# Another order for the first batch's steps, and nine unread products before the first expert tile

## The chip, the cores and the metric

The kernel runs on one core of a Trainium2 chip. The core has TensorE (PE, matrix products and transposes, with its weight loads shown apart as PEld), VectorE (DVE), ScalarE (ACT) and GpSimd (POOL). SyncE (SP) issues all the DMAs of this kernel. Every engine works through its own list of instructions in order and waits where a semaphore tells it to. The metric is the device time of one execution in microseconds (us).

## The reference, cut to what matters

Inputs are `q`, `k`, `v` of 8 batches x 8 heads x 576 rows x 64, `p` of 8 x 8 x 32 x 64, and the weights `w_a`, `w_b` (512 x 1536) and `w_out` (1536 x 512), all float32.

```python
p_packed = sm_attn(p, k, v)            # first scores: p @ k, softmax, times v
out = sm_attn(q, p_packed, p_packed)   # second scores: q @ pp, softmax over 32, times pp
x = out.transpose(0, 2, 1, 3).reshape(4608, 512)
return (x @ w_a) * (x @ w_b) @ w_out
```

## The kernel before

**Batches.** The eight batches are worked off one after the other. A batch has two attention stages, each in two halves (`e` = 0 and 1), and then the feed-forward part. Instead of forming the attention output, the kernel multiplies `pp` (the packed result of the first softmax) by a chunk of `w_a` and `w_b` ("pp @ w", `g_tiles`, L332), and multiplies that by the second softmax's weights `a2` (`mm1`, L351). There are six chunks of two f-tiles, so twelve f-tiles (`ft`) in a batch. Every operand of L351 is split into a high and a low part (`a_hi`, `a_lo`, `ghi`, `glo`), and three of the four products of parts are made, 12 matmuls for each half of an f-tile. ACT copies the first half out of PSUM (L363), DVE multiplies it with the second (L366), ACT and POOL split the result (L370, L86). Then `mm2` (L377) multiplies by `w_out`.

**The first scores** of batch 0 need k turned: five loads-and-turns `k0` to `k4` (`turn_first`), where `k0`, `k1` come from the first load (part 0), `k2`, `k3` from the second (part 1) and `k4` from the third (part 2), the same for q. A turn is four (for `k4`, `q4` eight) PE transposes into a bank and a copy by DVE or ACT; the string `TURN` says which. `S0`, `S1` are the score products of the two halves (L247), `r0`, `r1` the next steps of their softmax (L253 to L287), `P0` turns `pp` (L236, L237).

**The second scores** are `s0` and `s1`, one step at each mention: 1 the products (L297), 2 a transpose and a maximum on DVE (L302, L304), 3 the subtraction (L307), 4 the exponential on ACT (L309), 5 the sums and the reciprocal on DVE (L312 to L314) and the multiplication (L315), 6 a transpose on DVE (L318) and the high part on ACT (L319), 7 the low part on DVE (L86, `a_lo`). Steps 3 and the multiplication of 5 run on `eng`, in batch 0 on DVE for `s0` and on POOL for `s1`.

**The weights** come as 36 pieces of 512 KB: 24 of `w_a` and `w_b`, 12 of `w_out`. A piece is converted in three steps: A (the high word, ACT, L189), B (the low word, L194 or L197, on ACT, DVE or POOL as the digit of `WAYS` says: 0, 1, 2), C (both joined, DVE, L200). Twelve buffers hold pieces; a C frees one and issues the next load. D splits a `w_out` piece (ACT L225, POOL L86). Pieces 0 to 3 make chunk 0, 4 to 7 chunk 1 and so on; C makes a `w_out` piece in one single buffer, `wo_f`, which D empties.

**The order** is written out by hand. `FIRST` is the order of the first DMAs, `START` the steps up to the first f-tile, and the strings of `PLAN_0` the steps that stand after each half f-tile of batch 0 (24 slots) and after its `w_out` rounds. `Lp`, `Lk`, `Lq`, `Lv` issue the loads of the next batch. `g` in `START` is pp @ w of the first chunk. Later batches follow `PLAN`, which the change leaves alone. The PSUM pool `m` that `bank_pair()` gives out has two buffers.

Of the kernel before, what the change touches and what calls it, by code (L numbers as in the profile page):

```python
# [19 lines left out]
def tile_packed_attn_gated_ffn(  # L20
# [20 lines left out]
    nc = tc.nc  # L41
    B, H, S, D = q.shape
# [29 lines left out]
    ident = const.tile([P, P], F32, name="ident")  # L72
# [12 lines left out]
    def lo_part(dst, src, hi, eng=nc.vector):  # L85
        return eng.tensor_tensor(out=dst, in0=src, in1=hi.bitcast(F32), op=ALU.subtract)  # L86

    def bank():
        return ps_x.tile([P, 512], F32, name="x")

    def bank_pair(s=False):
        return ps_s.tile([P, 2, 512], F32, name="s") if s else ps_m.tile([P, 2, 512], F32, name="m")

    def work(b, name, shape, tag=None):
        if b == 0:
            return scratch.tile(shape, F32, name=name)
        return wk.tile(shape, F32, name=tag, bufs=2 if tag == "t1" else 1)
# [17 lines left out]
    def turn(key, b, i):  # L115

        t = nats.pop((key, b, i))
        xT = ld.tile([P, R, HS], F32, name=f"xT{i}")
        nc.vector.transpose(out=xT.rearrange("p h t -> p (h t)"), in_=t.rearrange("p h x d -> p (h x d)"))  # L119
        xTs.setdefault((b, key), []).append(xT)  # L120
# [3 lines left out]
    firsts = {}  # L124
# [12 lines left out]
    def turn_first(key, n):  # L137

        if (0, key) not in xTs:
            pool = scratch if key == "q" else ld  # L140
            xTs[0, key] = [pool.tile([P, R, HS], F32, name=f"xT{i}") for i in range(2)]
        copy = (nc.vector.tensor_copy, nc.scalar.copy)[int(TURN["kq".index(key) * 5 + n])]
        x = bank_pair()[:, 0, :] if n in (2, 3) else bank()
# [36 lines left out]
    def xT_cols(b, key, u, h, cols=slice(0, HS)):  # L180
        return xTs[b, key][h // R][64 * u:64 * u + 64, h % R, cols]
# [49 lines left out]
    def turned(dst, src, back=0):  # L231

        tp = bank()
        cols = src.rearrange("p e d -> p (e d)")
        for i in range(2):
            nc.tensor.transpose(tp[:, P * i:P * i + P], cols[:, 64 * (i ^ back):64 * (i ^ back) + P], ident)  # L236
        nc.vector.tensor_copy(out=dst.rearrange("p i r j -> p (i r j)"), in_=tp[:, 0:2 * P])  # L237
# [52 lines left out]
    def stage2(b, e):  # L290

        TU = 2 * XH
        hi, lo = (t[:, e, :].rearrange("p (x u l) -> p u x l", u=2, l=TL) for t in (a2_hi, a2_lo))
        x = bank_pair(b == 1 or e == 0)
        for r in range(R):
            for u in range(2):
                nc.tensor.matmul(  # L297
                    out=x[J * r:J * r + J, u, 0:HS], lhsT=ppT[64 * u:64 * u + 64, 1 if u ^ e else 2 * (b % 2), r, :],
                    rhs=xT_cols(b, "q", u, 2 * r + e), start=True, stop=True)
        yield  # L300
        s2 = work(b, f"s2_{e}", [P, TU, J], "t1")
        nc.vector.transpose(out=s2.rearrange("p (u x) j -> p u (x j)", u=2), in_=x[:, :, 0:HS])  # L302
        mx = sm.tile([P, TU], F32, name="mx")
        nc.vector.tensor_reduce(out=mx, in_=s2, axis=AX, op=ALU.max)  # L304
        yield
        eng = nc.gpsimd if b or e else nc.vector
        eng.tensor_tensor(out=s2, in0=s2, in1=mx.unsqueeze(2).broadcast_to([P, TU, J]), op=ALU.subtract)  # L307
        yield
        nc.scalar.activation(out=s2, in_=s2, func=AF.Exp, scale=scale)  # L309
        yield  # L310
        sum2 = sm.tile([P, TU], F32, name="sum2")
        nc.vector.tensor_reduce(out=sum2, in_=s2, axis=AX, op=ALU.add)  # L312
        nc.vector.tensor_scalar(out=sum2, in0=sum2, scalar1=1e-9, scalar2=None, op0=ALU.add)
        nc.vector.reciprocal(out=sum2, in_=sum2)  # L314
        eng.tensor_tensor(out=s2, in0=s2, in1=sum2.unsqueeze(2).broadcast_to([P, TU, J]), op=ALU.mult)  # L315
        yield
        a2f = work(b, f"a2f_{e}", [P, 2, XH, TL], "t2")
        nc.vector.transpose(out=a2f.rearrange("p u x l -> p (u x l)"), in_=s2.rearrange("p x j -> p (x j)"))  # L318
        nc.scalar.copy(out=hi, in_=a2f)  # L319
        yield  # L320
        lo_part(lo, a2f, hi)
        yield
# [97 lines left out]
    def emit(b, plan, tasks={}):  # L420

        for name in plan.split():
            if name in tasks:
                next(tasks[name], None)
                continue
            if name in "ABCD":
                convert(name)
                continue
            what, e = name[:-1], int(name[-1])
            n = b + (e // 2 if b or what[0] == "L" else 0)  # L430
            if n >= B:
                continue
            if what == "S":
                if e == 0:
                    st[b] = [stage1(b, 0), stage1(b, 1), stage2(b, 0), stage2(b, 1)]
                next(st[b][e])
            elif what == "s":
                next(st[b][2 + e], None)
            elif what == "r":
                next(st[b][e], None)  # L440
            elif what == "T":
                turned(pT, p_nat.pop(n))
            elif what == "P":
                turned(ppT[:, b % 2:b % 2 + 2], pp.pop(b), b % 2)
            elif what in ("k", "q"):
                turn(what, n, e % 2) if b else turn_first(what, e)
            elif what == "Lk":
                load(k, "k", n, e % 2)
            elif what == "Lq":
                load(q, "q", n, e % 2)  # L450
            elif what == "Lv":
                load_v(n, e % 2)
            elif what == "Lp":
                load_p(n)

    st = {}

    FIRST = ("p0 k0 k1 k2 q2 q0 v0 q1 v1 w1 w1 w1 w1 w1 w1 w1 w1 w1 w1 w1")
    START = ("T0 k0 k4 k1 k3 k2 q0 S0 S1 r0 q1 r1 r1 r0 r0 r1 r0 q2 r1 q3 P0 q4 A s0 A B s0 s0 B s1 s0 B s1 A s1 "
             "s0 C B Lp2 A C s1 s1 B A B B C B A C A s0 s1 s0 C Lk2 C B g A Lv2 A A C A B C B s1 C B A B Lk3 C A "  # L460
             "s1")
    WAYS = ("000000022220202120112012011200110102")
    TURN = ("1001111101")

    PLAN = (" | S0 | r0 |  | r0 | r0 |  | r0 Lv1 |  | S1 | r1 | q0 Lk2 | r1 |  |  | r1 q1 Lk3 |  | r1 Lv2 |  |  | "
            "T2 P0 |  |  | s0 s0 s1 g s0 |  | s1 | Lp4 s0 s1 s1 k2 | s0 | s0 | s1 s0 | s1 Lq2 | s1 | k3 Lq3")
    PLAN = dict(enumerate(PLAN.split("|")))
    PLAN_0 = ("B | C C | C A B A | C C A B B | A C A | k0 | A | B Lq0 B B | B C A C T0 A | C Lp2 C k1 | B A A | S0 "
# [3 lines left out]
    PLAN_0 = dict(enumerate(PLAN_0.split("|")))  # L472

    pieces = [(c, n) for c in range(NC) for n in range(4)] + [(NC, f) for f in range(NFT)]
# [2 lines left out]
    def load_pieces(n):  # L477

        for _ in range(n):
            if unloaded and len(raws) + len(wo_hi) + len(wo_f32) < NFT:  # L480
                c, r = unloaded.pop(0)
                if c < NC:
                    load_w(c, r)
                else:
                    load_wout(r)

    def convert(x):

        if x == "D":
            if wo_f32:  # L490
                split_wout(wo_f32.pop(0))
                load_pieces(2)
            return
        if not to_do[x]:
            return
        c, n = to_do[x].pop(0)
        if (c, n) not in raws:
            load_pieces(1)
        raw = raws[c, n]
        if x == "A":  # L500
            high_word(raw)
        elif x == "B":
            low_word(raw, int(WAYS[pieces.index((c, n))]))
        else:
            assert len(to_do["A"]) <= len(to_do[x]) and len(to_do["B"]) <= len(to_do[x])
            if c < NC:
                i, rr = divmod(n, 2)
                both_words(w_ab[:, c, 2 * rr:2 * rr + 2, 2 * P * i:2 * P * i + 2 * P], raw)
            else:
                t = sm.tile([P, DO], F32, name="wo_f32", bufs=1)  # L510
                both_words(t, raw)
                wo_f32.append(t)
            del raws[c, n]
            load_pieces(2)

    def next_g(b):

# [4 lines left out]
    ep(tc.manual_schedule(engines={ET.PE, ET.DVE, ET.Activation, ET.Pool, ET.SP}))  # L522
    for name in FIRST.split():
        what, i = name[0], int(name[1])
# [9 lines left out]
    tasks = {"g": next_g(0)}  # L534
    emit(0, START, tasks)
    drain(tasks["g"])
# [6 lines left out]
    for b in range(B):  # L543
        plan = dict(PLAN if b else PLAN_0)
        slot, tasks = [0], {"g": next_g(b + 1)}
# [73 lines left out]
```

## Time and profile before

| | |
|---|---|
| median of 3 runs | 748.11 us (747.31 to 749.12) |
| the profiled execution | 747.04 us |
| its span, first to last instruction | 745.3 us |
| busy in the span | PE 719.9 (97%), DVE 308.8 (41%), ACT 281.4 (38%), POOL 214.1 (29%) |
| mean granted clock of TensorE | 0.993 |

Busy is the time in which an engine had an instruction under way; for PE that is not its peak rate, since matmuls overlap. The time outside the span is 1.74 us. The shares are averages over a start in which PE waits a lot and a long rest in which it does not.

### The profile page before, as it was taken

Reading aid. Unit: us, or ns where it says so; the run is one execution under the profiler, and the core shown is the slowest. Engines: PE = TensorE matmul, PEld = TensorE weight load, DVE = VectorE, ACT = ScalarE, POOL = GpSimd, SP = SyncE. Lnnn points to the kernel's source line nnn. Section 1 sums busy time; section 2 is a strip of 40 time slices with the busy share of each in tenths; the row PEclk is TensorE's granted clock in tenths of the full one; section 3 lists DMA queues with packets and bytes.
Section 4 is the critical chain, followed back from the end, with each engine's and each line's share of the span. In section 5 each row is a group of like instructions: output and inputs, shape, how many; then the busy total and the mean of one; then the engine's idle time right before and its main releaser. Section 6 shows DMA issues by size and latency. Waiting matters only on the chain.

```text
span 745.3 us, 13719 instructions
## 1 busy us (share of the span) xinstructions
PE 719.9 (97%) x5844; PEld 602.9 (81%) x5844; DVE 308.8 (41%) x487; ACT 281.4 (38%) x494; POOL 214.1 (29%) x155
## 2 busy tenths in 40 slices
PE   5589899999999999999999999999999999999998
PEld 4278777888888888889788897888888888888887
DVE  2898856355303553244702446045520455123200
ACT  3777743444114531344203542055311553034300
POOL 0395754334103340133301333033400334023300
PEclk9799999999999999999999999999999999999999
DMA  8999952432510414014230242314050100100011
GB/s 255 362 255 256 284 100 54 88 67 54 92 41 24 71 43 91 30 45 90 47 74 15 55 80 47 76 33 73 24 106 29 33 1 2 43 15 1 1 29 43
DMA packets 171005, 58.30 MB, mean 78 GB/s; under 512 B 140608, under 2 KB 158784, under 8 KB 170944
## 3 DMA queue, kind: packets, MB, share of 16 engines
q1 hardware_dynamic: 170944, 57.43, 31.6%
q8 instruction: 46, 0.75, 0.4%
q14 instruction: 15, 0.12, 0.0%
HBM read 47.97 MB, written 9.44 MB: 77 GB/s over the span
## 4 chain that ended last, share of the span: by engine, by line
PE 91%; DVE 3%; DMA 1%; POOL 1%; issue 1%; ACT 1%; SPq 0%; DVEq 0%; POOLq 0%; ACTq 0%
PE m L377 40%; PE m L351 39%; PE x L332 6%; PE s L281 1%; PE s L247 1%; DVE w_ab L200 1%; PE s L297 1%; DMA kn<-in_k_dram 1%; PE s L271 1%; POOL wo L86 1%; DMA raw<-in_moe_w_b_dram 1%; DVE wo_f L200 1%; PE x L236 0%; PE m L297 0%; PE m L147 0%
## 5 line engine op out<-in xcount | busy, mean ns | idle before, releaser
L377 PE MATMUL m<-wo,h_hi 128*128 128x512 f32 (+1 forms) x888 | 268.8, 385 | 0.8 <-DVE asb L366 0.8
L86 POOL TENSOR_TENSOR h_lo<-asb,h_hi 128x576 fp32r<-128x576 f32 x96 | 138.6, 1444 | 411.5 <-ACT h_hi L370 411.3
L377 PEld LDWEIGHTS m<-wo,h_hi 128*128 128x128 f32 x888 | 164.2, 188 | 40.0 <-DVE t L302 5.0
L366 DVE TENSOR_TENSOR asb<-m,asb 128x576 f32<-128x576 f32 x96 | 72.6, 756 | 279.9 <-PE m L351 277.5
L351 PE MATMUL m<-a_hi,ghi 128*128 128x288 f32 x768 | 171.0, 304 | 2.4 <-ACT asb L363 1.7
L377 PE MATMUL m<-wo,h_lo 128*128 128x512 f32 (+1 forms) x444 | 170.4, 384 | 0.0
L351 PE MATMUL m<-a_lo,ghi 128*128 128x288 f32 x768 | 163.9, 295 | 0.9 <-DVE a_lo L86 0.9
L351 PEld LDWEIGHTS m<-a_hi,ghi 128*128 128x128 f32 x768 | 122.1, 188 | 39.7 <-issue 16.8
L351 PE MATMUL m<-a_hi,glo 128*128 128x288 f32 x768 | 133.4, 295 | 1.0 <-DVE glo L86 1.0
L351 PEld LDWEIGHTS m<-a_lo,ghi 128*128 128x128 f32 x768 | 123.5, 188 | 1.1 <-DVE a_lo L86 1.1
L370 ACT CAST h_hi<-asb 128x576 fp32r<-128x576 f32 x96 | 64.7, 674 | 143.0 <-DVE asb L366 143.0
L351 PEld LDWEIGHTS m<-a_hi,glo 128*128 128x128 f32 x768 | 112.7, 188 | 1.2 <-DVE glo L86 1.2
L377 PEld LDWEIGHTS m<-wo,h_lo 128*128 128x128 f32 x444 | 83.4, 188 | 16.7
L86 DVE TENSOR_TENSOR glo<-x,ghi 128x512 fp32r<-128x512 f32 x96 | 61.7, 684 | 52.7 <-ACT ghi L338 52.7
L363 ACT COPY asb<-m 128x576 f32<-128x576 f32 x96 | 61.6, 641 | 39.2 <-PE m L351 31.5
L332 PE MATMUL x<-w_ab,ppT 64*32 64x512 f32 x768 | 57.9, 606 | 7.9 <-DVE w_ab L200 7.9
L412 ACT COPY asb<-m 128x512 f32<-128x512 f32 x24 | 14.1, 587 | 134.2 <-PE m L377 133.4
L338 ACT CAST ghi<-x 128x512 fp32r<-128x512 f32 x96 | 51.4, 588 | 5.9 <-PE x L332 5.9
L119 DVE STREAM_TRANSPOSE xT<-nat 128x1152 f32<-128x1152 f32 x28 | 38.3, 1367 | 0.0
L412 ACT COPY wo_f<-m 128x512 f32<-128x512 f32 x11 | 6.5, 588 | 55.4 <-PE m L377 55.4
L332 PEld LDWEIGHTS x<-w_ab,ppT 64*32 64x32 f32 x768 | 13.6, 106 | 15.9 <-issue 12.3
L194 POOL TENSOR_SCALAR raw<-raw 128x512 uint32<-128x512 uint32 x11 | 23.7, 2157 | 0.9
(106 smaller groups left out, 407.2 us busy)
## 6 DMA issues: line engine op xcount, KB each, us to landing
nat<-in_k_dram SPq DMA_DIRECT2D x56, 144.0 KB
nat<-in_q_dram SPq DMA_DIRECT2D x56, 144.0 KB
vt<-in_v_dram SPq DMA_DIRECT2D x28, 256.0 KB
raw<-in_moe_w_a_dram SPq DMA_DIRECT2D x12, 512.0 KB
raw<-in_moe_w_b_dram SPq DMA_DIRECT2D x12, 512.0 KB
raw<-in_moe_w_out_dram SPq DMA_DIRECT2D x12, 512.0 KB
out_dram<-asb SPq DMA_DIRECT2D x17, 256.0 KB
out_dram<-wo_f SPq DMA_DIRECT2D x10, 256.0 KB
```

The costliest lines, as they stand in the source:

```text
L86: return eng.tensor_tensor(out=dst, in0=src, in1=hi.bitcast(F32), op=ALU.subtract)
L119: nc.vector.transpose(out=xT.rearrange("p h t -> p (h t)"), in_=t.rearrange("p h x d -> p (h x d)"))
L194: (nc.vector if way == 1 else nc.gpsimd).tensor_scalar(out=low, in0=low, scalar1=2.0 ** -29, scalar2=7.0, op0=ALU.mult, op1=ALU.min)
L200: nc.vector.scalar_tensor_tensor(out=dst.bitcast(U32), in0=raw[..., 1], scalar=3, in1=raw[..., 0], op0=ALU.logical_shift_left, op1=ALU.bit ...
L332: nc.tensor.matmul(out=gps[e][J * r:J * r + J, :], lhsT=ppT[rows, 2 * (b % 2), r, :], rhs=w_ab[rows, c, r, :], start=True, stop=True)
L338: nc.scalar.copy(out=ghi[:, e], in_=gps[e])
L351: nc.tensor.matmul(out=ps[:, half, 0:HS], lhsT=gt[:, kt, i, :], rhs=at[:, kt, HS * half:HS * half + HS], start=(n == 0 and kt == 0), stop= ...
L363: nc.scalar.copy(out=asb, in_=pa[:, :, 0:HS])
L366: nc.vector.tensor_tensor(out=asb, in0=pb[:, :, 0:HS], in1=asb, op=ALU.mult)
L370: nc.scalar.copy(out=hh, in_=flat)
L377: nc.tensor.matmul(out=o[:, cols], lhsT=ht[:, c0:c0 + P], rhs=wt[:, cols], start=(ft == 0 and n == 0), stop=(ft == NFT - 1 and n == 2))
L412: nc.scalar.copy(out=ob, in_=o)
```

## The change

`FIRST`, `START`, `PLAN_0`, `TURN` and `WAYS` get other contents, the engine of the subtraction and multiplication of the second softmax is read from a string `SUBS` (batch 0: half 0 on POOL, half 1 on DVE; batch 1 as before), and a step `W` issues nine products of the identity with the first 512 columns of the first k load as it came from memory, between the products of the second scores and `g`. Nobody reads their result.

```diff
-        eng = nc.gpsimd if b or e else nc.vector
+        eng = nc.vector if b < 2 and SUBS[2 * b + e] == "1" else nc.gpsimd
...
+            if name == "W":
+                warm()
                 continue
...
-    FIRST = ("p0 k0 k1 k2 q2 q0 v0 q1 v1 w1 w1 w1 w1 w1 w1 w1 w1 w1 w1 w1")
-    START = ("T0 k0 k4 k1 k3 k2 q0 S0 S1 r0 q1 r1 r1 r0 r0 r1 r0 q2 r1 q3 P0 q4 A s0 A B s0 s0 B s1 s0 B s1 A s1 "
-             "s0 C B Lp2 A C s1 s1 B A B B C B A C A s0 s1 s0 C Lk2 C B g A Lv2 A A C A B C B s1 C B A B Lk3 C A "
-             "s1")
-    WAYS = ("000000022220202120112012011200110102")
-    TURN = ("1001111101")
+    FIRST = ("p0 k0 k2 k1 q0 v0 q1 v1 q2 w1 w1 w1 w1 w1 w1 w1 w1 w1 w1 w1")
+    START = ("T0 k0 k4 k1 k3 k2 q0 S0 S1 r0 r1 q1 r1 r0 r0 r1 r0 q2 r1 q3 q4 P0 s0 B s1 W A s0 B A A s0 s0 B s1 C "
+             "A s1 B s0 C s1 A s1 C B B Lp2 C A B A s0 s1 B C B B s0 B g A C A A s1 Lv2 Lk2 C C A A C B B Lk3 C s1")
+    WAYS = ("000000022220202120012012011200010010")
+    TURN = ("0001110101")
+    SUBS = ("0100")
...
-    PLAN_0 = ("B | C C | C A B A | C C A B B | A C A | k0 | A | B Lq0 B B | B C A C T0 A | C Lp2 C k1 | B A A | S0 "
-              "B | B A C r0 | r0 C | B A | C C C | B r0 D A | C S1 A D B | A Lq1 C B B D | r1 C | A D A | r0 | C A "
-              "D B | B r1 B B r1 A B C Lv1 |  |  | q0 C q1 r1 D A Lk2 A | C D P0 Lv2 C D | s0 s0 Lk3 A C | T2 s1 s1 "
-              "D | B s0 | D A | B s0 s0 C | k2 D s1 Lp4 s0 k3 | s1 s1 |  | s0 Lq2 Lq3 s1 s1")
+    PLAN_0 = ("A | C C | B A B A | B C B C C | A A | C | B | C B A T0 k0 Lp2 A | A A B B C Lq0 | C C k1 | A B A | "
+              "S0 B | B A r0 | C C C | B A Lq1 |  | C C B r0 r0 D A A | S1 C D | B C B B A D | r1 C | A A D | r0 T2 "
+              "|  | q0 B r1 C B D r1 C |  | A | D B C Lv1 A r1 | A B D Lk2 B C B q1 D Lk3 A A P0 | C s0 s0 D C Lp4 "
+              "A B | s1 s0 | Lv2 | D | s0 s1 s0 | k2 s0 s1 C k3 | s1 |  | Lq2 D s0 s1 s1 Lq3 s1")
...
+    def warm(n=9):
+
+        x = bank_pair()[:, 0, :]
+        t = firsts["k", 0].rearrange("p h t -> p (h t)")
+        for _ in range(n):
+            nc.tensor.matmul(out=x, lhsT=ident, rhs=t[:, 0:512], start=True, stop=True)
```

## Rows read from the trace of the kernel before

**Rows 1.** Stretches of the span: length, each engine's busy time, clock, DMA share, GB/s

```profile
22.69:36.97 14.28, 5.39 (x48) 1.27 (x49) 13.00 (x20) 11.12 (x21) 5.62 (x4) 0.64 1.01 355
...
43.78:64.85 21.07, 20.71 (x187) 17.22 (x179) 20.05 (x27) 15.75 (x28) 16.23 (x9) 1.00 0.98 265
...
92.68:745.30 652.62, 649.37 (x5135) 548.00 (x5135) 242.13 (x385) 220.40 (x382) 167.05 (x122) 1.00 0.23 49
```

**Rows 2.** Timeline of PE, the start to the second scores: start, length, instruction

```profile
10.26 1.11 PE L147 MATMUL x<-ident,kn 128*128 128x128 f32 x4
11.17 1.91 PE L147 MATMUL m<-ident,kn 128*128 128x128 f32 x8
12.88 0.73 PE L147 MATMUL x<-ident,qn 128*128 128x128 f32 x4
13.53 0.77 PE L247 MATMUL s<-xT,pT 64*32 64x288 f32 x10
...
22.69 0.86 PE L297 MATMUL s<-xT,ppT 64*32 64x288 f32 x16 [0.35 <-ACT xT L154]
...
24.33 0.67 PE L297 MATMUL m<-xT,ppT 64*32 64x288 f32 x3 [0.31 <-issue]
```

**Rows 3.** Chain of waits that ended last: start, length, what; to 23 us

```profile
3.79 5.38 DMA kn<-in_k_dram
...
14.72 0.77 DVE nmx L253
...
16.60 0.47 ACT xT L149
...
22.37 0.28 ACT xT L154
```

**Rows 4.** Timeline of DVE, then of POOL, from the second softmax on

```profile
29.74 1.28 DVE L200 SCALAR_TENSOR_TENSOR w_ab<-raw 128x512 uint32<-128x512 uint32 x2
...
32.11 2.18 DVE L200 SCALAR_TENSOR_TENSOR w_ab<-raw 128x512 uint32<-128x512 uint32 x2
...
36.40 1.72 DVE L200 SCALAR_TENSOR_TENSOR w_ab<-raw 128x512 uint32<-128x512 uint32 x2
...
39.25 1.27 DVE L200 SCALAR_TENSOR_TENSOR w_ab<-raw 128x512 uint32<-128x512 uint32 x2
...
32.34 1.40 POOL L315 TENSOR_TENSOR s<-s,sum 128x576 f32<-128x576 f32 x1 [3.65 <-ACT raw L189]
33.83 11.32 POOL L194 TENSOR_SCALAR raw<-raw 128x512 uint32<-128x512 uint32 x5
```

**Rows 5.** Timeline of PE and ACT, pp @ w of the first chunk, first f-tile

```profile
32.89 3.39 PE L332 MATMUL x<-w_ab,ppT 64*32 64x512 f32 x16 [7.88 <-DVE w_ab L200]
36.97 0.54 PE L351 MATMUL m<-a_hi,ghi 128*128 128x288 f32 x2 [0.69 <-ACT ghi L338]
...
41.25 0.53 PE L351 MATMUL m<-a_lo,ghi 128*128 128x288 f32 x2 [0.87 <-DVE a_lo L86]
...
43.78 0.53 PE L351 MATMUL m<-a_hi,ghi 128*128 128x288 f32 x2
...
35.02 1.33 ACT L319 CAST a_hi<-a2f 128x576 fp32r<-128x576 f32 x2 [2.19 <-DVE a2f L318]
```

**Rows 6.** Timelines of SP and ACT: loads of pieces 21 on, and their first use

```profile
57.25 0.76 SPq L210 DMA_DIRECT2D raw<-in_moe_w_a_dram  x1
...
63.30 0.68 ACT L197 ACTIVATE raw<-raw 128x512 uint32<-128x512 uint32 x1
```

**Rows 7.** Timeline of PE, two later waits, and of DVE before the second

```profile
82.83 0.53 PE L351 MATMUL m<-a_hi,ghi 128*128 128x288 f32 x2 [1.32 <-ACT asb L363]
...
92.68 0.50 PE L377 MATMUL m<-wo,h_hi 128*128 128x512 f32 x1 [0.78 <-DVE asb L366]
...
90.06 1.90 DVE L200 SCALAR_TENSOR_TENSOR wo_f<-raw 128x512 uint32<-128x512 uint32 x1 [1.02 <-POOL wo L86]
91.89 0.74 DVE L366 TENSOR_TENSOR asb<-m,asb 128x576 f32<-128x576 f32 x1
```

More of the change, by code (lines that the diff above doesn't have):

```diff
@@ L425, in emit @@
                 continue
+            if name == "W":
+                warm()
+                continue
             if name in "ABCD":
@@ L467, in tile_packed_attn_gated_ffn @@
     PLAN = dict(enumerate(PLAN.split("|")))
-    PLAN_0 = ("B | C C | C A B A | C C A B B | A C A | k0 | A | B Lq0 B B | B C A C T0 A | C Lp2 C k1 | B A A | S0 "
[3 rows of a table removed]
+    PLAN_0 = ("A | C C | B A B A | B C C B C | A A | C | B | C B A T0 k0 Lp2 A | A A B B C Lq0 | C C k1 | A B A | "
[3 rows of a table added]
     PLAN_0 = dict(enumerate(PLAN_0.split("|")))
```

## The prediction

> **What bounds the kernel now.** I read the table of stretches first. From 92.68 us on, PE is busy 649.37 of 652.62 us [rows 1]: the last of batch 0 and seven batches whose plan is not touched. Nothing can be won there; an advance reached by then goes whole into the end, and so does a delay. Between the start of the second scores (22.69) and the first f-tile (36.97) PE is busy 5.39 of 14.28 us and DVE 13.00, so DVE sets the pace and PE waits for it; the mean granted clock is 0.64 there. From 43.78 to 64.85 PE has 20.71 of 21.07 us and DVE 20.05: both nearly full, so DVE can't catch up on much [rows 1]. The chain of waits shows what sets the start: the third k load, which lands at 3.79 + 5.38 = 9.17, then turns and scores on PE, the maximum on DVE at 14.72, a copy on ACT between two exponentials (16.60, 0.47), and at 22.37 the copies of `q4` [rows 3]. Last the timelines: pp @ w waits 7.88 us for the third conversion C, and the first f-tile stops again for `ghi` and for the second low part, at 41.25 [rows 5]. So I follow one checkpoint after another and ask how much earlier each is reached.
>
> **The start.** Before, `k4` waits for the third k load, and `k1`, which is behind it on PE, begins at 10.26 [rows 2]. With the small load ahead of the second one, `k4` can fill the idle time that was there, and `k1` waits for the second load, which then lands last of the three. Whatever their order, the three were all there at 9.17 [rows 3]; so `k1` begins at about 9.3, 0.95 earlier. Eight transposes took 11.17 to 12.88, 0.214 us each, and the four of `q0` 0.65 together (12.88 to 13.53), so the rate doubled within them [rows 2]. If the clock rises at the same moment, `q0` is slower by 0.2: the first scores begin 0.75 earlier, at 12.8. I take 0.8, since they then also stop less for a copy. Bounds: 0.4, if the second load is late by as much; 2.2, if the clock rises as early as `k1`, which saves 0.107 on each of the 12 to 16 transposes. The q load that moves behind v is first used at `q4`, whose copies came at 22.37, 13 us after the k loads, and the piece loads behind it keep their place: nothing.
>
> `q1`'s copy goes from ACT to DVE, behind both maxima. It stood between the exponentials for 0.47 [rows 3]; the second maximum takes over as the limit, so I take 0.35 (0 to 0.47). `P0` behind `q4` means that the copy of `ppT` on DVE ends this part and not `q4`'s copies: 0.2 lost (0 to 0.5). The second scores begin 0.8 + 0.35 - 0.2 = 0.95 earlier, at 21.75. Call that moment X; before it is 22.69.
>
> **The nine products.** A float32 product shows as two matmuls (the 8 of L332's loops are x16 [rows 5]), so W is 18 matmuls of 512 columns. No row has one. Turns of the same full array take 0.214 for 128 columns at what their later doubling shows to be the 1.2 GHz level, so 0.107 at 2.4 and four times that, 0.43, for 512: 7.7 us. I take 8.0, with starts between; at the lower level it would be 15.4. W follows the products of `s1`, which before ended at 24.33 + 0.67 = X + 2.3 [rows 2], so it ends at X + 10.3. The cover is the softmax on DVE: the fourth C ends at X + 10.9 (below), and pp @ w needs the third and fourth. W's bank was read long before (`q3`'s copy), and the first f-tile gets that of `s1`, which DVE has read by then. What W gives is the clock: the second-scores stretch showed 0.64 [rows 1], and pp @ w took 3.39 us in it. But ACT had both `a_hi` casts to do until 35.02 + 1.33 = 36.35, and pp @ w was over at 36.28 [rows 5], so the faster products are worth about 0 on the path; they keep the earlier f-tile from starting at half clock. I cost W at 0. The casts end 2.06 behind the fourth C (36.35 - 34.29), and pp @ w takes at most half of 3.39 at the higher level, so W may end as late as X + 10.9 + 2.06 - 1.7 = X + 11.3; past that it costs what it exceeds it by.
>
> **The second softmax.** DVE has the same steps up to the fourth C. Before, this pair of conversions took 2.18 (32.11 to 34.29 = X + 11.6), while the pair at 29.74 took 1.28: the second one ran beside POOL's multiplication (32.34, 1.40) and ended after it [rows 4]. After, POOL multiplies half 0 and begins when DVE has just begun its second conversion, as at 32.34, and behind that stands half 1's sum; DVE then does half 1's subtraction and multiplication. That saves 0.9, and 0.2 comes back because POOL's conversions, which began right behind its multiplication (33.83), now begin sooner and run beside the third and fourth C (pairs beside them: 1.72 and 1.27, against 1.28 alone [rows 4]). Sum 0.7; bounds 0, if the multiplication catches another conversion, and 0.9. POOL is slower at the two steps, but half 1's steps on DVE cover it: its result is due only after the fourth C. The fourth C: X + 10.9 = 32.65.
>
> **The first f-tile.** Before, two pairs of conversions (36.40, 1.72, and 39.25, 1.27) stood on DVE between the transposes and the second low part, for which PE stood still at 41.25 [rows 4, 5]. After, two conversions, one pair less: 1.3 (bounds 0, if ACT's copies end last, and 1.7). So the checkpoint at 41.25 comes 0.95 + 0.7 + 1.3 = 2.95 earlier.
>
> **What is late next.** The conversions that were put off stand, four in a row, ahead of the first gate (L366). PE wants the bank that it frees only in the second half of the next f-tile, 1.0 for pp @ w and 1.6 behind the first; four conversions take 2.6 to 3.4 by the pairs. I take 0.3 lost (0 to 0.8). SP: piece 17 goes ahead of the k and v loads of batch 1, and pieces 21 on stand behind the second k load as before; 21 was issued at 57.25 and first used at 63.30 [rows 6]. All of that SP list is freed by conversions that come 1 to 2 us earlier, and a use that comes 3 earlier eats some of the 6 between: 0.2 lost (0 to 1). Of the later waits the one at 82.83 stays, since a D still stands ahead of ACT's copies. The one at 92.68 came from a conversion of 1.90 ahead of the last gate (90.06, 91.89) [rows 7]; its slot is now empty, so most of 0.78 goes: 0.6 (0 to 0.78).
>
> **The sum.** 2.95 - 0.3 - 0.2 + 0.6 = 3.05, say 3.1. The profiled execution took 747.04 (span 745.3 and 1.74 around it): 743.9. The median of the runs shown is 1.07 above it, so the median after should be 748.11 - 3.1 = 745.0.
>
> **Rivals.** *DVE gives it back.* Where DVE is 20.05 of 21.07 us busy [rows 1], PE can keep only what DVE itself gained, 0.95 + 0.7, and reordering conversions gains DVE nothing: 1.65, or 0.8 less with the gate late by its bound: 746.5 to 747.3. For it speaks DVE's share, against it that PE's waits there were short.
> *Nothing arrives.* The pieces come too late, or the chain through the single `wo_f` buffer (C on DVE, D on ACT and POOL) sets when batch 0 ends and doesn't move: within 1 us of 748.1. Against it: C there follows a gate, and the gate follows PE.
> *Slower: W is not hidden.* If W runs at the 1.2 GHz level, 15.4, it ends at X + 17.7, 6.4 us after its limit, and 3.3 remain after what was won: 751.4. For it speaks that the clock did fall in this stretch; against it, that PE idled 7.88 us in it, and that W starts without a gap behind the scores. It decides once W ends after X + 11.3 + 3.1 = X + 14.4.
> *More.* The clock rises at `k1` (1.4 more), or the waits behind 43.78 shrink as well: 743.6 and below.
> *The clock rule.* Before, the rate of turns doubled while PE had done nothing but turns from 10.26 on [rows 2]. If turns did not raise the clock, the first scores and `q1`'s turns would begin at half rate, about 1 us more by the 0.65 to 0.77 that such groups take: 746.0. The Trainium skill's page "TensorE: Matmul & The Clock Gate", section on PE-mode transpose, says that transposes do not bring the full clock; by that rule the sum would be 746.0, but these rows do not agree with it.
>
> **How the numbers follow.** Forecast (2.1 to 4.1 won) 0.46, more 0.10, DVE gives it back 0.22, the clock rule 0.03, nothing 0.10, slower 0.09. About 0.2% or 1.5 us is what a measurement of this kernel can tell from no change. Faster by more: 0.46 + 0.10 + half of 0.22 + 0.02 = 0.69; within: the other half, 0.01 and 0.10 = 0.22; slower: 0.09. The range, 743.0 to 747.6, leaves out the slower case, half of nothing and some of more.
>
> **What would show it.** `k1`'s turns at 9.3; the second scores near 21.7; 18 matmuls of 0.43 to 0.49 behind them, over before pp @ w, and a clock of 1.0 throughout; the fourth C near 32.7; the first f-tile near 35 and its second low part near 38; no wait over 0.3 at the first `mm2` product. A pp @ w that stands behind W, a first gate after 42, or ACT waiting for piece 21 would make it wrong.

## The result, and the profile after

The changed kernel takes 739.62 us in the median of 4 runs (739.47 to 741.35), beside 747.93 us of the kernel before (747.31 to 749.12): a ratio of 0.9892 with an interval of 0.9873 to 0.9911. So it is 8.3 us faster, where 3.1 were forecast and 743.0 was the lower end of the range. The profiled executions stand 7.34 apart (747.04 and 739.7, spans 745.3 and 737.9). One run of experiment 5, of 1189.78 us, stands far off all others and moves the median of that experiment by 0.14.

The table of stretches of the kernel after, at the stretches of [rows 1]: from the second scores to the first f-tile, from the second f-tile to the start of the seventh, and the last 652.62 us.

```profile
core 0: us, PE busy (x) PEld busy (x) DVE busy (x) ACT busy (x) POOL busy (x), PEclk, DMA share, GB/s
22.08:35.09 13.01, 11.36 (x67) 4.35 (x67) 11.96 (x21) 10.60 (x20) 7.47 (x5) 1.00 1.06 387
40.35:60.16 19.81, 19.69 (x182) 17.06 (x178) 17.52 (x27) 16.27 (x29) 16.14 (x9) 1.00 1.04 254
85.28:737.90 652.62, 649.43 (x5136) 547.91 (x5134) 241.24 (x385) 222.96 (x386) 164.47 (x121) 1.00 0.24 51
```

The last stretch, counted back from the end, is PE's 649 of 652.62 us as before, so the advance was there when it began. The second one is 1.26 us shorter than before's 21.07, though nothing was forecast for it. The granted clock is 1.00 in all three; before it was 0.64 in the first.

The timeline of PE after, at the checkpoints of [rows 2, 5]: start, length, instruction, and in brackets the wait ahead of it.

```profile
9.32 1.11 PE L147 MATMUL x<-ident,kn 128*128 128x128 f32 x4
...
11.93 1.06 PE L147 MATMUL x<-ident,qn 128*128 128x128 f32 x4
12.92 1.00 PE L247 MATMUL s<-xT,pT 64*32 64x288 f32 x24
13.74 0.90 PE L247 MATMUL m<-xT,pT 64*32 64x288 f32 x24
...
22.08 0.72 PE L297 MATMUL s<-xT,ppT 64*32 64x288 f32 x16 [0.61 <-DVE ppT L237]
...
23.90 7.99 PE L524 MATMUL m<-kn,ident 128*128 128x512 f32 x18
32.04 1.57 PE L332 MATMUL x<-w_ab,ppT 64*32 64x512 f32 x16 [0.15 <-DVE w_ab L200]
35.09 0.54 PE L351 MATMUL m<-a_hi,ghi 128*128 128x288 f32 x2 [1.48 <-ACT ghi L338]
...
37.68 0.53 PE L351 MATMUL m<-a_lo,ghi 128*128 128x288 f32 x2 [0.27 <-DVE a_lo L86]
...
40.35 0.53 PE L351 MATMUL m<-a_hi,ghi 128*128 128x288 f32 x2
```

L524 is `warm()`: 18 matmuls in 7.99 us. They fill the time in which pp @ w waited 7.88 before, and it starts 0.15 behind them. The waits of [rows 7] have no counterpart: behind 37.68 the largest wait of PE in batch 0 is one of 0.12, ahead of 43.92.

The timelines of DVE and POOL after, which answer to [rows 3, 4] (the first line is the maximum of the first scores, 14.72 before), the last two lines being POOL's and SP's (piece 21, [rows 6]):

```profile
14.12 0.76 DVE L253 TENSOR_REDUCE nmx<-s 128x1 f32<-128x576 f32 x1 [1.25 <-PE s L247]
...
31.22 1.28 DVE L200 SCALAR_TENSOR_TENSOR w_ab<-raw 128x512 uint32<-128x512 uint32 x2
...
37.54 3.43 DVE L200 SCALAR_TENSOR_TENSOR w_ab<-raw 128x512 uint32<-128x512 uint32 x4
40.90 0.74 DVE L366 TENSOR_TENSOR asb<-m,asb 128x576 f32<-128x576 f32 x1
...
28.54 1.41 POOL L315 TENSOR_TENSOR s<-s,sum 128x576 f32<-128x576 f32 x1 [2.83 <-DVE sum L314]
...
54.50 0.76 SPq L210 DMA_DIRECT2D raw<-in_moe_w_a_dram  x1
```

The third and fourth C (31.22) now take 1.28, the multiplication on POOL (28.54) being over before they begin; the four conversions that were put off (37.54) stand ahead of the first gate at 40.90.

The account below is taken from PE's starts in the two timelines (only the fourth C's end is DVE's); "c2" is pp @ w of the third chunk, and so on. Its last column is what the prediction's sum put there.

| stretch | before | after | gained | forecast |
|---|---|---|---|---|
| to the second scores (X) | 22.69 | 22.08 | 0.61 | 0.95 |
| X to the end of the fourth C | 11.60 | 10.42 | 1.18 | 0.7 |
| to the second low part | 6.96 | 5.18 | 1.78 | 1.3 |
| to c2 (50.35, after 47.31) | 9.10 | 9.63 | -0.53 | -0.3 |
| to c3 (58.97, 55.12) | 8.62 | 7.81 | 0.81 | -0.2 |
| to c4 (68.23, 63.55) | 9.26 | 8.43 | 0.83 | 0 |
| to c5 (76.87, 72.19) | 8.64 | 8.64 | 0 | 0 |
| to the first `mm2` product (90.97, 84.85) | 14.10 | 12.66 | 1.44 | 0 |
| to batch 1's first pp @ w (126.12, 118.78) | 35.15 | 33.93 | 1.22 | 0.6 |
| to the end (745.3, 737.9) | 619.18 | 619.12 | 0.06 | 0 |

Up to the second low part 3.57 came instead of 2.95, and behind it 3.83 instead of 0.1. The larger half of the surprise lies where the forecast had left the profile as it was. Of the 1.22, 0.3 is no gain: the two turns of p for batch 2, which took 0.31 of PE there before (110.65 to 110.96), now stand in the stretch ahead, at 80.93.

Two of the four waits that are gone are in [rows 7]. The other two are the 0.36 at 55.38 and c3, which took 1.91 instead of 1.09 within PE's own row. The timelines of the kernel before up to c3 (PE, DVE, POOL), and then around the wait at 82.83 (DVE, POOL, ACT):

```profile
55.38 0.53 PE L351 MATMUL m<-a_hi,ghi 128*128 128x288 f32 x2 [0.36 <-ACT asb L363]
...
58.97 1.91 PE L332 MATMUL x<-w_ab,ppT 64*32 64x512 f32 x16
...
56.87 2.53 DVE L200 SCALAR_TENSOR_TENSOR w_ab<-raw 128x512 uint32<-128x512 uint32 x2
59.33 0.41 DVE L237 COPY pT<-x 128x256 f32<-128x256 f32 x1
...
57.07 1.78 POOL L86 TENSOR_TENSOR h_lo<-asb,h_hi 128x576 fp32r<-128x576 f32 x1 [1.75 <-ACT h_hi L370]
...
78.71 1.90 DVE L200 SCALAR_TENSOR_TENSOR wo_f<-raw 128x512 uint32<-128x512 uint32 x1 [1.11 <-POOL wo L86]
...
78.63 1.44 POOL L86 TENSOR_TENSOR h_lo<-asb,h_hi 128x576 fp32r<-128x576 f32 x1
...
80.65 0.62 ACT L225 CAST wo<-wo_f 128x512 fp32r<-128x512 f32 x1 [1.59 <-DVE wo_f L200]
...
82.13 0.65 ACT L363 COPY asb<-m 128x576 f32<-128x576 f32 x1
```

In both places a conversion on DVE begins beside a `TENSOR_TENSOR` of POOL and ends 0.55 after that has ended (59.40 after 58.85, 80.61 after 80.07): 1.78 for the second of the pair and 1.90, where 0.65 to 0.69 is usual. Behind the first stands the copy of `pT` (59.33), which frees the bank that c3 wants (its weight loads wait 0.7 for that copy); behind the second stands D on ACT (80.65), and behind D the copy L363 (82.13) for which PE waits at 82.83. The same in the kernel after (DVE, POOL, ACT):

```profile
53.16 0.42 DVE L237 COPY pT<-x 128x256 f32<-128x256 f32 x1
...
69.39 0.69 DVE L200 SCALAR_TENSOR_TENSOR wo_f<-raw 128x512 uint32<-128x512 uint32 x1
...
72.96 0.73 DVE L200 SCALAR_TENSOR_TENSOR wo_f<-raw 128x512 uint32<-128x512 uint32 x1 [0.34 <-POOL wo L86]
...
73.40 1.58 POOL L86 TENSOR_TENSOR h_lo<-asb,h_hi 128x576 fp32r<-128x576 f32 x1 [0.47 <-ACT h_hi L370]
...
73.73 0.62 ACT L225 CAST wo<-wo_f 128x512 fp32r<-128x512 f32 x1 [0.41 <-DVE wo_f L200]
...
75.33 0.64 ACT L363 COPY asb<-m 128x576 f32<-128x576 f32 x1
```

Here the copy of `pT` comes 2 us before c3 (55.12), the conversion at 72.96 begins 0.44 ahead of POOL's `h_lo` and takes 0.73, and D follows it at once. One conversion of 1.90 is left in batch 0's f-tiles, at 79.80 beside the `h_lo` of 79.73; no wait of PE follows it.

### The profile page after: what moved, and what is told of

Read it like the earlier page. It is cut to its first block, busy times and chain, and to the rows that moved or that the text cites. A ratio compares the mean times of both kernels' runs of the same rounds, so it can differ in the third digit from the quotient of the medians.

```text
span 737.9 us, 13756 instructions
## 1 busy us (share of the span) xinstructions
PE 724.8 (98%) x5862; PEld 606.0 (82%) x5862; DVE 302.4 (41%) x487; ACT 282.6 (38%) x495; POOL 212.5 (29%) x154
## 4 chain that ended last, share of the span: by engine, by line
PE 95%; DVE 2%; DMA 1%; ACT 1%; issue 0%; SPq 0%; DVEq 0%; ACTq 0%
PE m L351 42%; PE m L377 40%; PE x L332 6%; PE s L281 2%; PE s L247 1%; PE s L271 1%; PE s L297 1%; DMA raw<-in_moe_w_b_dram 1%; DMA kn<-in_k_dram 1%; PE x L236 0%; DVE w_ab L200 0%; PE x L147 0%; PE m L297 0%; PE m L147 0%; SPq L177 0%
## 5 line engine op out<-in xcount | busy, mean ns | idle before, releaser
L363 ACT COPY asb<-m 128x576 f32<-128x576 f32 x96 | 61.6, 641 | 36.7 <-PE m L351 29.0
L332 PE MATMUL x<-w_ab,ppT 64*32 64x512 f32 x768 | 55.4, 597 | 0.2 <-DVE w_ab L200 0.2
L315 POOL TENSOR_TENSOR t<-t,sum 128x576 f32<-128x576 f32 x14 | 16.5, 1178 | 25.0 <-DVE sum L314 25.0
L189 ACT ACTIVATE raw<-raw 128x512 f32<-128x512 f32 x36 | 23.1, 683 | 0.1
```

The costliest lines, as they stand in the source:

```text
L189: nc.scalar.activation(out=high, in_=high, func=AF.Prelu, scale=2.0 ** -112, alpha=-2.0 ** 32)
L332: nc.tensor.matmul(out=gps[e][J * r:J * r + J, :], lhsT=ppT[rows, 2 * (b % 2), r, :], rhs=w_ab[rows, c, r, :], start=True, stop=True)
L363: nc.scalar.copy(out=asb, in_=pa[:, :, 0:HS])
```

## The experiments

Theory A was: the start, the second softmax and the first f-tile gave some 3.5, with W as what keeps the clock up, and the rest comes from moves of steps in batch 0 that take away the later waits: `T0` to slot 7, one C (piece 22) to slot 13, and one C (piece 28) with its D to slot 23. Against it stood that the later waits went because all before them came earlier, so that the plan is worth nothing by itself, and that W is worth nothing, or nearly everything. Each kernel was timed in 5 rounds against the kernel before, whose median was 748.11 us for the first group (`e1` to `e4`), 748.02 for the second (`e5` to `e8`) and 748.28 for the third. X differs from execution to execution: 21.80 to 22.56 in nine profiles with the new order of the first loads and turns (mean 22.33), 22.45 to 23.53 in five with the old one (mean 22.99). So stretches are compared, not moments. "More than the change" below is counted from its 739.62, which was timed beside 747.93; by the distance from the kernel before of their own group these losses are 0.1 to 0.35 smaller. The intervals of 1, 4, 9 and 10 lie almost wholly within the change's (0.9873 to 0.9911), so for these four the time alone does not show a loss; what they show rests on the waits in their traces, one trace each.

**1. After without W.**

```diff
-... q4 P0 s0 B s1 W A s0 B A A
+... q4 P0 s0 B s1 A s0 B A A
```

> The changed kernel without the nine products; nothing else differs. Theory A (the order of the conversions carries the gain, the products only keep the clock): the granted clock falls behind the second scores, pp @ w of the first chunk takes about 1.7 us more and ends behind ACT's casts, and a part of the first f-tile runs at the lower level: 1.0 to 1.7 us above the changed kernel, 740.6 to 741.3. Theory B (the products are what I missed): 3 us or more above it, 742.6 or later. Theory C (the products change nothing): 739.4 to 739.9.

Measured: 740.87 us (740.11 to 741.65), ratio 0.9896 [0.9881, 0.9911], 1.25 more than the change. Its table of stretches, from X to the first f-tile and from there to c1 (the second chunk's pp @ w):

```profile
22.56:35.81 13.25, 4.30 (x49) 1.09 (x49) 12.14 (x21) 10.56 (x20) 7.53 (x5) 0.67 1.05 386
35.81:41.43 5.62, 5.62 (x25) 5.46 (x25) 5.62 (x8) 4.79 (x9) 5.46 (x3) 0.55 0.97 312
```

The first f-tile starts nearly as early (X + 13.25 against X + 13.01), but it runs at a granted clock of 0.55, mostly the 1.2 GHz level, and takes 5.62 up to c1 where the kernel after takes 4.11. Of the 1.75 lost from X to c1, 0.5 comes back up to c2 (7.60 against 8.11), and by the medians 1.25 is left, as A said (1.07 against its own group's kernel before). That is the worth of W here as far as it can be told; 3 or more, theory B, is excluded.

**2. The new start with the old plan** (PLAN_0 and WAYS of before, slot 0 as "A B").

```diff
-    PLAN_0 = ("A | C C | B A B A | B C C B C | A A | C | B | C B A T0 k0 Lp2 A | A A B B C Lq0 | ...
+    PLAN_0 = ("A B | C C | C A B A | C C A B B | A C A | k0 | A | B Lq0 B B | B C A C T0 A | ...
```

> The first loads, the start, the engines of the second softmax and the nine products of the changed kernel, with the plan of the first batch's f-tiles and the engines of the conversions of the kernel before (one A more in slot 0, since the new start has made one less). Theory A: the start's advance of 3.4 us at the second f-tile stays, and the later waits (0.4, 0.8, 1.3 and 0.8 us in the profile before) come back: 743.3 to 744.5. Theory D (an earlier start alone lets the later waits vanish): 739.6 to 740.6.

Measured: 745.09 (745.0 to 745.93), ratio 0.9959 [0.9946, 0.9971], 0.6 above the expectation. PE's waits, in its timeline:

```profile
51.12 0.53 PE L351 MATMUL m<-a_hi,ghi 128*128 128x288 f32 x2 [0.55 <-DVE asb L366]
53.34 0.53 PE L351 MATMUL m<-a_hi,ghi 128*128 128x288 f32 x2 [0.36 <-ACT asb L363]
56.93 1.91 PE L332 MATMUL x<-w_ab,ppT 64*32 64x512 f32 x16
...
80.79 0.53 PE L351 MATMUL m<-a_hi,ghi 128*128 128x288 f32 x2 [1.34 <-ACT asb L363]
90.67 0.73 PE L377 MATMUL m<-wo,h_hi 128*128 128x512 f32 x2 [0.77 <-DVE asb L366]
```

c1 comes at X + 17.12, as after (before: X + 20.07). Then all four later waits of before are back, with a fifth (51.12): from c1 to the end it takes 703.67, where before took 702.54 and after 698.70. So an earlier start does not take them away, and that rival falls.

**3. The old start with the new plan** (before, with PLAN_0 and WAYS of after: the edit of 2 the other way).

> The start of the kernel before, without the nine products, and the plan of the f-tiles and the engines of the conversions of the changed one. Theory A: the later waits go, 3 to 4 us gained without the start's: 744 to 745. Theory D: the plan alone is worth less than 1 us: 747 to 748.

Measured: 745.19 (744.64 to 746.74), ratio 0.996 [0.9947, 0.9973]: 2.9 by the plan alone, a little less than A's 3 to 4. The four waits are gone, but there is a new one ahead of 65.57. ACT and SP, in their timelines:

```profile
62.77 0.68 ACT L189 ACTIVATE raw<-raw 128x512 f32<-128x512 f32 x1 [2.68 <-DMA raw<-in_moe_w_a_dram]
...
57.98 0.77 SPq L210 DMA_DIRECT2D raw<-in_moe_w_a_dram  x1
```

SP issues piece 21 at 57.98, 3.5 later than after's 54.50, and ACT stands still 2.68 for it; PE's part is 1.43. The halves give 3.0 and 2.9 of 8.3, since each needs the other: with the old plan a new start gives 1.1 back behind c1, and with the old start the new plan runs into piece 21.

**4. After, with the C of piece 22 back where it was.**

```diff
-| C C C | B A Lq1 |  | C C B r0 r0 D A A |
+| C C | B A Lq1 | C | C C B r0 r0 D A A |
```

> The changed kernel with one conversion C (piece 22) moved back from slot 13 to slot 15, where the kernel before has it, so that on VectorE three conversions stand in a row again behind the gate of the eighth f-tile. Theory A: the third of them meets the low part of that f-tile on GpSimd, takes 1.9 us and not 0.7, the chain through the single buffer of w_out pieces gets late, and PE waits 1.0 to 1.5 us ahead of the eleventh f-tile: 740.6 to 741.1. Rival: the wait went because all came earlier, and the place of this conversion does not matter: 739.4 to 739.9.

Measured: 741.02 (740.53 to 741.59), ratio 0.9902 [0.9888, 0.9915], 1.4 more than the change. From c5 to the first `mm2` product it is 13.70 instead of 12.66. The timelines of DVE, POOL and PE:

```profile
70.24 1.92 DVE L200 SCALAR_TENSOR_TENSOR wo_f<-raw 128x512 uint32<-128x512 uint32 x1
...
69.91 1.70 POOL L86 TENSOR_TENSOR h_lo<-asb,h_hi 128x576 fp32r<-128x576 f32 x1 [2.47 <-DMA raw<-in_moe_w_out_dram]
...
79.58 0.53 PE L351 MATMUL m<-a_hi,ghi 128*128 128x288 f32 x2 [0.54 <-DVE asb L366]
```

The third conversion meets `h_lo` and takes 1.92, where the kernel after has 0.69 (69.39). PE's wait is smaller than A's 1.0 to 1.5 and stands half an f-tile later: ahead of the eleventh f-tile, where before had 1.32, it is 0.11, and in the middle of it 0.54, for DVE's gate.

**5. Before, with W behind the products of `s1`.**

```diff
-... B s1 s0 B s1 A s1 s0 C B Lp2
+... B s1 W s0 B s1 A s1 s0 C B Lp2
```

> The kernel before with the nine products alone, behind the products of the second scores. Theory A: they keep the clock at 2.4 GHz until pp @ w of the first chunk; the order of the kernel before leaves the first f-tile waiting for VectorE, so only what ran at the lower level is won, 0.3 to 1.5 us: 746.6 to 747.8. Theory B (the products carry the gain): 743 or less. Rival: they delay pp @ w and cost time: 749 or more.

Measured: 748.32, ratio 1.0004 [0.9995, 1.0013]: nothing, and A's gain was missed. Its table of stretches, from X to the first f-tile, and a part of that f-tile:

```profile
22.45:36.66 14.21, 12.05 (x67) 4.52 (x67) 12.93 (x20) 11.12 (x21) 5.54 (x4) 1.00 1.01 355
...
40.81:44.22 3.41, 3.21 (x18) 2.64 (x26) 2.12 (x4) 1.42 (x3) 3.33 (x2) 0.50 0.87 163
```

The clock is full through pp @ w, but the first f-tile, in before's order, still stops for DVE (1.10 at 38.55, 0.89 at 41.02), and the clock is 0.50 from 40.81 to 44.22, where PE works almost without a stop. In the profile of before it was 0.50 from 26.77 to 37.02, most of which PE spent waiting, and the first f-tile ran at 1.00. W moved the fall of the clock into the f-tile, it did not remove it.

**6. After, with the second softmax's halves on the engines of before.**

```diff
-    SUBS = ("0100")
+    SUBS = ("1000")
```

> The changed kernel with the engines of the second softmax as in the kernel before: half 0 on VectorE, half 1 on GpSimd. Theory A: the multiplication on GpSimd falls later, onto the third and fourth C, which it holds up by about 0.9, and GpSimd's conversions start later: first f-tile 0.7 to 1.2 us later, 740.3 to 740.9. Rival: the engines do not matter, the order alone does: 739.4 to 739.9.

Measured: 742.08 (741.32 to 742.57), ratio 0.992 [0.9907, 0.9934]: 2.5 more than the change, more than A allowed. DVE's and POOL's timelines:

```profile
31.47 2.19 DVE L200 SCALAR_TENSOR_TENSOR w_ab<-raw 128x512 uint32<-128x512 uint32 x2
...
31.70 1.41 POOL L315 TENSOR_TENSOR s<-s,sum 128x576 f32<-128x576 f32 x1 [3.05 <-ACT raw L189]
```

The pair takes 2.19 again beside POOL's multiplication, as in [rows 4]; the first f-tile comes at X + 13.86, 0.85 later. Another 0.98 goes between c3 and c4 (9.41 against 8.43), where batch 1's first scores wait; that one A did not have. From X to the end the profile shows 1.80 of the 2.5.

**7. Before, with the C of piece 22 early** (slot 15 to 13).

```diff
-| r0 C | B A | C C C | B r0 D A |
+| r0 C C | B A | C C | B r0 D A |
```

> The kernel before with one conversion C (piece 22) moved from slot 15 to slot 13, nothing else. Theory A: two conversions stand behind the gate of the eighth f-tile and not three, the second begins before the low part on GpSimd, and the wait of 1.3 us ahead of the eleventh f-tile goes or shrinks: 746.6 to 747.2. Rival: the place of this conversion matters only in the changed order: 747.7 to 748.3.

Measured: 747.26 (746.71 to 748.72), ratio 0.9992 [0.9981, 1.0003]: unclear by the time, and just above A's range. In the trace the wait of 1.32 is down to one of 0.32 at 88.60, and c5 to the first `mm2` product takes 12.92 instead of 14.10; but the half-level stretch of the clock is longer in this profile (26.96 to 44.02; before 26.77 to 37.02), and c1 comes at X + 21.27 instead of X + 20.07.

**8. After, with 18 unread products instead of nine.**

```diff
-    def warm(n=9):
+    def warm(n=18):
```

> The changed kernel with eighteen unread products in place of nine, 7.9 us more on PE. Theory A: the nine ended about 1.3 us before they would have cost anything, so the other nine cost 6 to 7 us: 745.6 to 746.6. Rival 1 (the nine already stand in the way of pp @ w): 7.9 us, 747.5. Rival 2 (what comes early at the first f-tile is lost behind it anyway): 743 or less.

Measured: 745.8 (744.87 to 746.48), ratio 0.9971 [0.9959, 0.9982], 6.2 more than the change. PE's timeline:

```profile
24.21 15.72 PE L524 MATMUL m<-kn,ident 128*128 128x512 f32 x36
```

pp @ w stands behind them up to 39.86. The first f-tile comes at X + 19.28, 6.27 later, for 7.73 more of unread products: nine had 1.46 to spare, which is the 1.48 that PE waits for `ghi` at 35.09.

**9. After, with the C of piece 28 one slot earlier again**, ahead of the last gate.

```diff
-|  | q0 B r1 C B D r1 C |
+| C | q0 B r1 B D r1 C |
```

> The changed kernel with one conversion C (piece 28) moved back from slot 23 to slot 22, ahead of the last gate of the first batch, as in the kernel before. Theory A: it meets the low part on GpSimd, takes 1.9 us and delays the gate, and PE waits 0.6 to 0.8 us ahead of the second product of the w_out part: 740.2 to 740.5. Rival: the wait was due to something else: 739.4 to 739.9.

Measured: 740.93 (740.3 to 741.31), ratio 0.9897 [0.9882, 0.9912], 1.3 more than the change. DVE and PE, in their timelines:

```profile
84.24 1.89 DVE L200 SCALAR_TENSOR_TENSOR wo_f<-raw 128x512 uint32<-128x512 uint32 x1 [0.67 <-POOL wo L86]
...
86.85 0.73 PE L377 MATMUL m<-wo,h_hi 128*128 128x512 f32 x2 [0.60 <-DVE asb L366]
```

The time is above A's range, but what A said is there: a conversion of 1.89 stands ahead of the gate (86.05) again, and the `mm2` product behind waits 0.60, as in [rows 7]. The rest need not be the edit's: this profile, whose X is the earliest of all (21.80), also waits for piece 21 (ACT 2.12, up to 60.63), as in experiment 3, and c3 to c4 takes 9.25 instead of 8.43.

**10. After, with `T0` and `Lp2` one slot later**, behind a C, as before.

```diff
-| C B A T0 k0 Lp2 A | A A B B C Lq0 |
+| C B A k0 A | A A B B C T0 Lp2 Lq0 |
```

> The changed kernel with T0 of batch 1 (two turns of p on PE and a copy on VectorE) moved back from slot 7 to slot 8, behind the conversion of piece 17, with the load of the next p behind it. Theory A: pp @ w of the fourth chunk needs the bank that this copy reads, and the copy stands behind a conversion: 0.5 to 0.9 us lost, 740.1 to 740.6. Rival: the copy's place does not matter: 739.4 to 739.9.

Measured: 741.28 (740.11 to 742.0), ratio 0.9902 [0.9888, 0.9915], 1.7 more. PE's and DVE's timelines:

```profile
55.41 2.11 PE L332 MATMUL x<-w_ab,ppT 64*32 64x512 f32 x16
...
55.97 0.41 DVE L237 COPY pT<-x 128x256 f32<-128x256 f32 x1
```

c3 waits inside its row for the copy of `pT`, and c3 to c4 takes 9.45 instead of 8.43. The rest, which puts the time above A's range, is not located.

**11. Before, with the three moves alone.**

```diff
-| B Lq0 B B | B C A C T0 A | ... | r0 C | B A | C C C | ... | r0 | C A D B | B r1 B B ...
+| T0 B Lq0 B B | B C A C A | ... | r0 C C | B A | C C | ... | r0 | A B | C D B r1 B B ...
```

> The kernel before with three of its steps moved and nothing else: T0 of batch 1 to the front of slot 7, one C (piece 22) from slot 15 to slot 13, and one C (piece 28) with the D behind it from slot 22 to slot 23. Theory A: these three moves take away the three later waits of the profile before (0.8, 1.3 and 0.8 us) and account for most of the new plan's worth: 745.2 to 746.2. Rival: the waits come back elsewhere as soon as one goes: 747 or more.

Measured: 745.2 (744.56 to 745.9), ratio 0.9956 [0.9943, 0.9968]: 3.1 won, as much as by the whole new plan on the old start (2.9, with 1.43 lost to piece 21). From c1 to the end it takes 699.43, against 702.54 before and 698.70 after: 3.11 of the 3.84 that the change gains there.

**12. Before, with the new order of loads and turns** (FIRST, TURN, `q1` behind `r1`, `P0` behind `q4`).

```diff
-... S0 S1 r0 q1 r1 r1 r0 r0 r1 r0 q2 r1 q3 P0 q4 A s0
+... S0 S1 r0 r1 q1 r1 r0 r0 r1 r0 q2 r1 q3 q4 P0 A s0
```

> The kernel before with the changed order of the first loads, the changed engines of the first copies, the copy of q1's turn behind both exponentials and the turn of pp behind q4; nothing else. Theory A: the second scores begin 0.6 to 0.95 us earlier and all of it stays: 747.0 to 747.5. Rival: the waits of the first f-tile take it back: 747.8 to 748.3.

Measured: 746.62 (745.71 to 747.99), ratio 0.9978 [0.997, 0.9987]: 1.7 won, twice what was expected. X is at 22.50 in its profile, and over all profiles the new order brings it 0.66 earlier. Where the other 1.0 lies stays open, the profiled execution being the slowest of its 11 runs.

## Why the prediction was wrong in size

**The step that failed** is "What is late next", with "Of the later waits the one at 82.83 stays, since a D still stands ahead of ACT's copies". The D does stand there, but what made it late was the conversion that feeds it, at 1.90 beside POOL's `h_lo`: this term was put at nothing, and with 1.44 it is the largest miss of the table. One C moved two slots lets these conversions begin ahead of `h_lo`; c5 to the first `mm2` product gained 1.44, and experiments 4 and 7 show 1.04 lost and 1.18 won there by that C. The same step had nothing for c3, whose wait hides inside a row of 1.91 that no bracket marks (0.83; experiment 10: 1.02), nor for the 0.36 at 55.38. With 1.22 instead of 0.6 behind the first `mm2` product, this step's 0.1 became 3.83. Experiment 11 shows that the three moves carry most of it; the rest of the new plan and of `WAYS` was not tried by itself.

The rival *DVE gives it back* judged DVE by its share, 20.05 of 21.07. Part of this share was conversions held by POOL, and the same work is shorter where it meets POOL less often. The groups of C in the kernel before, over the whole execution (busy, mean ns of one):

```profile
L200 DVE SCALAR_TENSOR_TENSOR w_ab<-raw 128x512 uint32<-128x512 uint32 x24 | 19.3, 831 | 0.6 <-POOL raw L194 0.4
L200 DVE SCALAR_TENSOR_TENSOR wo_f<-raw 128x512 uint32<-128x512 uint32 x12 | 13.2, 1104 | 5.9 <-POOL wo L86 5.9
```

and in the kernel after:

```profile
L200 DVE SCALAR_TENSOR_TENSOR w_ab<-raw 128x512 uint32<-128x512 uint32 x24 | 16.9, 738 | 0.0
L200 DVE SCALAR_TENSOR_TENSOR wo_f<-raw 128x512 uint32<-128x512 uint32 x12 | 10.4, 866 | 8.7 <-POOL wo L86 8.5
```

The same 36 conversions take 27.3 us instead of 32.5.

**The start.** `k1`'s turns came at 9.32, 0.94 earlier, as said. But the rate of PE doubled at nearly the same moment in both kernels: before within the turns of `q0` (at 13.2), after within the first scores (at 13.4). So `q0`'s turns lost 0.34 (11.93 to 12.92, before 12.88 to 13.53) and not 0.2: the first scores came 0.61 earlier and their maximum 0.60 (14.12, before 14.72), where 0.8 was set. `q1`'s copy gave 0.36, as set: the turns of the second half's exponentials come 0.96 earlier (16.90, before 17.86). `P0` behind `q4` took 0.35 back where 0.2 was set. The sum is 0.61, not 0.95. Of the *clock rule* this bears out that the scores began at half rate, but not its price of 1: from the first scores to the maximum both kernels take 1.2. The granted clock of this time reads 1.00 and does not show the rise.

**The second softmax** was right in mechanism and too small in its term: 1.18 against 0.7, so that in spite of X's shortfall the fourth C came 1.79 earlier against 1.65. The 0.2 that was to come back did not: the pair at 31.22 takes 1.28 beside POOL's conversions. Experiment 6 shows the place: 0.85 up to the first f-tile.

**The first f-tile** gave 1.78, over its bound of 1.7. Before, the two pairs took 1.72 and 1.27; after, two single conversions of 0.65 and 0.69 (33.77, 36.27), so 1.65 on DVE where a price of 1.3 for a pair was set. No experiment takes this move by itself.

**The nine products** were right: 0.44 each, hidden, over 9.8 behind X (limit 11.3), and, by experiment 8, 1.46 to spare. They "keep the earlier f-tile from starting at half clock", and experiment 1 gives that its price, 1.75 up to c1 and some 1.1 to 1.25 in the medians. Experiment 5 shows that they are worth nothing where the f-tile behind them stops again.

**The first gate** lost 0.53 where 0.3 (0 to 0.8) was set, and piece 21 lost nothing where 0.2 was: ACT began with it at 59.17, with no wait. Experiments 3 and 9 show how little was left there.

The profiled executions differ by 7.3 and the medians by 8.3, with the interval reaching from 6.7 to 9.5. The half-level stretch of the clock took 10.24 us in the profile of before, and 13.65 or 17.07 in those of experiments 3, 7, 11 and 12, which begin as before does or nearly so. But that the timed runs of before hold longer stretches does not explain the difference: of the 46 timed beside the experiments, the 17 with a mean granted clock of 0.993, that of the profiled execution (747.04 us; 10.24 us at half level take 0.007 off the mean), have a mean time of 748.4, and the other 29 of 748.2. What makes the profiled execution of before short stays open.

## What to carry to other kernels

Price a reordering by every wait behind it, those inside a long row too (a group of 1.91 where its like takes 1.09), and ask of each which instruction upstream was stretched and by what: here 3.1 us hung on three steps, moved by one or two places. An engine's high busy share is no proof that it can't catch up when some of its instructions are held by another engine. Before adding unread products that keep TensorE's clock up, look at what follows them: here they paid where the f-tile behind ran almost through and not where it stopped again, and only as long as they ended before what they wait beside.

## What the runs showed of the hardware

A conversion on DVE (`SCALAR_TENSOR_TENSOR`, two inputs in SBUF) that began beside a `TENSOR_TENSOR` of POOL took up to 1.9 us instead of 0.65 and ended 0.55 after POOL's: 34.29 after 33.74 [rows 4], 80.61 after 80.07 before, 72.16 after 71.61 in experiment 4. In all 14 profiles it is 0.54 to 0.57 for each conversion that began at least 0.07 behind POOL's, wherever in it. One that began 0.44 ahead of POOL's took 0.73, and at 49.12 before one that began 0.04 ahead took 0.69. The Trainium skill's page "SBUF — State Buffer", section "SBUF: two separate sides", says that such an instruction and a GpSimd one that reads SBUF exclude each other for a whole instruction, whichever comes first. The rows above agree for the `TENSOR_TENSOR`. They do not for POOL's `TENSOR_SCALAR`: five of them ran in 11.75 us without a gap (from 30.03 after), and the pair of conversions at 31.22, beside them, took 1.28. Others beside them took longer (the pair at 36.40 before 1.72, the four at 37.54 after 3.43), but none stood still until POOL's had ended.

The clock fell to its half level (0.50) in experiment 5 at 40.81, among stops of 1.48, 1.10 and 0.89 in that f-tile; in the kernel after, with stops of 1.48 and 0.27 there, it stayed at 1.00. And the moment at which PE's rate first doubled in these two profiles (13.2 before, 13.4 after) did not move with `k1`'s turns, which began 0.94 earlier.
